# Attention and two expert layers on one core: value rows of two units summed on GpSimd, and eight group sums moved in VectorE's queue

## The chip, the cores and the metric

The program runs on one core of a Trainium2 chip. A time is the device time of one execution, in microseconds (us). The engines go by the profile's names: PE is TensorE's matmuls and PEld its weight loads, DVE is VectorE, ACT is ScalarE, POOL is GpSimd, and SP is SyncE, which here only issues transfers. Each engine works through its own queue of instructions in the order that was fixed when the program was built; an instruction that waits holds up all that stand behind it on its engine.

## The reference

Attention over 4 batches, 8 heads, 576 positions, 64 columns per head, is the sum of two parts. The first works on means over groups of four positions (144 groups) and is repeated four times along the sequence; the second sees only keys less than four positions away. The result goes through a dense layer (512 to 2048 to 512 with a squared ReLU) and through eight experts of which each token takes the best one.

```python
q_d = q.reshape(B, H, Sd, factor, D).mean(axis=3)   # k_d and v_d alike, factor 4
out_d = sm_attn(q_d, k_d, v_d)
out_up = np.repeat(out_d, factor, axis=2)
mask = np.abs(pos[:, None] - pos[None, :]) < factor
...
out_local = np.matmul(attn, v)
return (out_up + out_local).astype(np.float32)
```

## The kernel before, in words

**Units.** A unit is one batch and one pair of heads: `attention(b, hp, ap, psa)`, lines 195 to 342, a generator that is driven step by step. Its steps, as far as they matter here: load q and k (L198); the group sums of q and k, two `tensor_reduce` on VectorE (L205); load the value windows and the grouped value rows `vr` (L212, L214), local scores on TensorE (L226), mask (L233); scores of the groups (L242), maximum (L253), subtraction on GpSimd (L254), exponential on ScalarE (L255); maxima and sums (L262 to L270), the reciprocals of the sums (L271), the multiplication by them on GpSimd (L272); transposes `pt` on TensorE (L288) and their copy (L291); transposes `pdt` (L300) and their copy (L306); the product `pu` with the grouped values (L316) and its copy `up` (L321); the product `po` with the value windows (L329); and `xT`, the sum of both (L335 on VectorE).

**Grouped values.** The mean over four value rows is made in one of two ways. For batches 1 to 3 GpSimd adds the four rows in two instructions (L295, L296), and `pu` takes 8 matmuls. For batch 0 nothing is added; `pu` runs over all four rows, 32 matmuls, and PSUM's accumulation makes the sum.

**Order.** Four sets of buffers exist; set i does batch 0 and then batch 1 of head pair i (`serial`, L810). `rounds` (L830) drives the four sets in turn, set i starting i rounds late, and lets in the first pieces of the weight conversion (`f64_split`, L380: ScalarE L389, VectorE L390, L392, L394, ScalarE L396, GpSimd L397). Four such pieces are written ahead of the end of batch 0, later ones behind it, two for each chunk of the dense layer at first (`wanted`, L867). The order that each engine's queue gets is made from this written order by a planner that places an instruction when its inputs are there by its own reckoning; `tc.issue_after(x)` makes it keep an instruction behind x in the queue of x's engine, and adds no wait.

**Slots.** `pt`, `pdt`, `pu` and `po` of a unit take turns in two PSUM slots that units 0 and 1 share; units 2 and 3 have two others in batch 0. `po` of unit 1 takes the slot that `xT` of unit 0 empties.

**What follows.** The dense layer's first product (L461) takes `xT` of all four units of batch 0, split into two parts (L447, L448). From then on its matmuls (L461, L484), the rest of the conversion and the units of batch 1 run interleaved (L902 and on).

```python
parts = [(j, g) for j in range(2) for g in range(GR if b == 0 else 1)]
for j, g in parts:
    for a in range(2):
        nc.tensor.matmul(
            pu[64 * a:64 * a + 64, 0, 0:SD],
            lhsT=vr[:, a, j, g, :], rhs=PdT[:, j, :, a, :],
            start=((j, g) == parts[0]), stop=((j, g) == parts[-1]))
```

Of the kernel before, what the change touches and what calls it, by code (L numbers as in the profile page):

```python
# [16 lines left out]
ALU = mybir.AluOpType  # L17
AX = mybir.AxisListType
# [7 lines left out]
def attn_moe_kernel(  # L26
# [13 lines left out]
    nc = tc.nc  # L40
# [5 lines left out]
    P = 128  # L46
    GR = 4
    SD = S // GR
# [25 lines left out]
    class Parts:  # L74
# [32 lines left out]
        out=psum4, in_=ident.rearrange("p (k e) -> p e k", k=KC)[:, 0:2 * E, :], axis=AX.X, op=ALU.add)  # L107
# [80 lines left out]
    for o in orders:  # L188
        nc.gpsimd.dma_start(out=o.rearrange("(p c) o -> p (c o)", p=P), in_=none)
    nc.gpsimd.dma_start(out=ytab[0:1, :].rearrange("o (p c) -> (o p) c", p=8),  # L190
                        in_=none[0:8, 0:YW // 8])

    xT = {}

    def attention(b, hp, ap, psa):
        n = f"{b}_{hp}"
        qkt = ap.tile([P, 2, S], F32, tag="qk", name=f"qk{n}", bufs=2)
# [3 lines left out]
        qk_d = ap.tile([P, 2, SD + 16], F32, tag="qkd", name=f"qkd{n}")  # L201
        if b == 0:
            nc.gpsimd.memset(qk_d[:, 0, SD:], 0.0)
        for i in range(2):
            nc.vector.tensor_reduce(  # L205
                out=qk_d[:, i, 0:SD], in_=qkt[:, i, :].rearrange("p (s g) -> p s g", g=GR),
                axis=AX.X, op=ALU.add)
            yield

        def values():  # L210
# [10 lines left out]
        for ip in range(5):  # L221
            for x in range(2):
                for a in range(2):
                    hb = (x + a) % 2
                    i = 2 * ip + hb
# [6 lines left out]
        for a in range(2):  # L232
            nc.vector.scalar_tensor_tensor(  # L233
                out=sm[:, :, a, :], in0=ps[:, a, 0:320].rearrange("p (i c) -> p i c", i=5),
# [16 lines left out]
        smv = sm.rearrange("p i a c -> p (i a) c")  # L251
# [9 lines left out]
        sums, inv = st[:, 0:13], st[:, 13:26]  # L261
# [3 lines left out]
        for i in range(3):  # L265
# [2 lines left out]
                                 accum_out=sums[:, 10 + i:11 + i])  # L268
        nc.vector.tensor_reduce(out=sums[:, 0:10], in_=smv, axis=AX.X, op=ALU.add)
        nc.vector.tensor_scalar(out=sums, in0=sums, scalar1=1e-9, scalar2=None, op0=ALU.add)  # L270
        nc.vector.reciprocal(out=inv, in_=sums)  # L271
        nc.gpsimd.tensor_mul(out=smv, in0=smv,  # L272
                             in1=inv[:, 0:10].unsqueeze(2).to_broadcast([P, 10, 64]))
        yield
        if b == 0:
            for i in range(3):
# [2 lines left out]
        else:  # L279
            nc.gpsimd.tensor_mul(out=sd, in0=sd,  # L280
                                 in1=inv[:, 10:13].unsqueeze(2).to_broadcast([P, 3, SD]))
# [8 lines left out]
        PT = ap.tile([P, 5, P], F32, tag="PT", name=f"PT{n}")  # L290
        nc.scalar.activation(out=PT.rearrange("p i r -> p (i r)"), in_=ptv, func=AF.Copy)  # L291
        yield
        if b > 0:
            vq = vr.rearrange("p a j g d -> p (a j) g d")
            nc.gpsimd.tensor_add(out=vq[:, :, 0:2, :], in0=vq[:, :, 0:2, :], in1=vq[:, :, 2:4, :])  # L295
            nc.gpsimd.tensor_add(out=vq[:, :, 0, :], in0=vq[:, :, 0, :], in1=vq[:, :, 1, :])  # L296
        pt = psa.tile([P, 2, 512], F32, tag="at", name=f"pdt{n}")
        for j in range(2):
            for bi in range(3):
                nc.tensor.transpose(out=pt[:72, j, P * bi:P * bi + P],  # L300
                                    in_=sd[:, bi, 72 * j:72 * j + 72], identity=ident)
        if b < 2:
            PdT = ap.tile([72, 2, 3, 2, 48], F32, tag="sm", name=f"PdT{n}")
        else:
            PdT = ap.tile([72, 2, 3, 2, 48], F32, tag="PdT", name=f"PdT{n}")
        nc.scalar.activation(  # L306
            out=PdT.rearrange("p j b a c -> p j (b a) c"),
            in_=pt[:72, :, 0:3 * P].rearrange("p j (x c) -> p j x c", c=64)[:, :, :, 0:48],
# [1 line left out]
        yield  # L310

        pu = psa.tile([P, 2, 512], F32, tag="at", name=f"pu{n}")
        parts = [(j, g) for j in range(2) for g in range(GR if b == 0 else 1)]
        for j, g in parts:
            for a in range(2):
                nc.tensor.matmul(  # L316
# [8 lines left out]
        for i in range(NW):  # L325
            bk, o, ln = i // 5, Q0[i] - SH * (i // 5), Q0[i + 1] - Q0[i]
            r = (i % 2) * 64 + Q0[i] - QS[i]
            for a in range(2):
# [7 lines left out]
            out=xt.rearrange("p (h s g) -> p h s g", h=2, g=GR),  # L336
            in0=po[:, :, 0:SH].rearrange("p h (s g) -> p h s g", g=GR),
            in1=up.rearrange("p (h s) -> p h s", h=2).unsqueeze(3).to_broadcast(
                [P, 2, SD // 2, GR]),
            op=ALU.add)  # L340
# [3 lines left out]
    def chain(units):  # L344

        gens = [attention(*u) for u in units]

        def go(i, n):
            for _ in range(n if i < len(gens) else 0):
                next(gens[i], None)  # L350
                yield

        yield from go(0, 4)
        for i in range(len(gens)):
            yield from go(i, 3)
            yield from go(i + 1, 3)
            yield from go(i, 2)
            yield from go(i + 1, 1)
            yield from go(i, 1)
            if len(gens) == 1:  # L360
                yield from gens[i]
            else:
                go_on = gens[i]
                next(go_on, None)
                yield
# [444 lines left out]
    def serial(units):  # L810
        gens = [attention(*u) for u in units]
        next(gens[0])
        yield
        for i, g in enumerate(gens):
            for n, _ in enumerate(g):
                if n == 2 and i + 1 < len(gens):
                    next(gens[i + 1])
                yield
# [83 lines left out]
    for s in range(len(seq) + LAG):  # L902
        if s < len(seq):
            sg, c, f = seq[s]
            j, n = f - SEGS[sg][1], SEGS[sg][2] - SEGS[sg][1]
# [52 lines left out]
    with tc.high_priority():  # L958
# [11 lines left out]
        for i in range(2):  # L970
            nc.gpsimd.indirect_dma_start(
                out=xg01[i][:], out_offset=None, in_=ytab[:],
# [6 lines left out]
    for o in orders:  # L979
        og = cv.tile([P, DM], I32, tag="tmp", name="og", bufs=TMPB).bitcast(F32)[:E * NTL // 2, 0:2 * P]  # L980
        nc.gpsimd.dma_start(out=og.rearrange("t (h p) -> t h p", h=2),
                            in_=o.rearrange("(t h p) o -> t h (p o)", h=2, p=P))
# [31 lines left out]
    for h in range(2):  # L1014
        nc.vector.tensor_sub(out=sh[:, h], in0=pov[:, h, :, 1:HT], in1=gih[:, h, :, 0:HT - 1])
        nc.vector.tensor_tensor(out=sh[:, h], in0=sh[:, h],
                                in1=star.unsqueeze(2).to_broadcast([P, E, HT - 1]),
                                op=ALU.mult)
        nc.vector.tensor_tensor(out=gih[:, h, :, 0:HT - 1], in0=pov[:, h, :, 0:HT - 1], in1=sh[:, h],
                                op=ALU.add)  # L1020
# [203 lines left out]
```

## Time and profile before

| | |
|---|---|
| median of 3 runs | 903.58 us (902.75 to 905.36) |
| the profiled execution | 903.22 us |
| its span, first to last instruction | 901.4 us |
| PE busy | 821.4 us, 91% of the span |
| DVE, ACT, POOL busy | 450.6, 395.3, 341.6 us |
| mean granted TensorE clock | 0.973 of full speed |

The profiled execution lies 0.36 us under the median; 1.8 us of it lie outside the span. The shares are means over stages that differ: batch 0's attention takes the first 67 us, after which the dense layer's matmuls run.

### The profile page before, as it was taken

The page shows a single profiled execution, that of the slowest core. Times are in us where ns is not written, and L with a number is a line of the kernel's source. Part 1 is how long each engine was busy: PE and PEld are TensorE (multiplying, and loading weights), DVE is VectorE, ACT ScalarE, POOL GpSimd, SP SyncE. Part 2 cuts the span into 40 slices and gives each one's busy share as a digit, 9 for nine tenths or more (in the row PEclk, how much of TensorE's full clock was granted, in tenths as well). Part 3 has the DMA queues.
Part 4 walks back from the last instruction along what each step waited for, and adds up shares of the span by engine and source line. Part 5 has one row for each costly group of instructions (what it writes and reads, how often), then busy time and mean ns, then how long its engine had stood idle before and what let it go on. Part 6 is the DMA issues. An engine that isn't in the chain of part 4 may idle for free. (4 is left out here: it accounts for less than half of the span.)

```text
span 901.4 us, 15844 instructions
## 1 busy us (share of the span) xinstructions
PE 821.4 (91%) x5983; PEld 695.4 (77%) x5983; DVE 450.6 (50%) x961; ACT 395.3 (44%) x899; POOL 341.6 (38%) x411
## 2 busy tenths in 40 slices
PE   4598979997899989999999999997799989999996
PEld 3386869886788878888988888775587767878785
DVE  8987585777354654353222224652743656434121
ACT  3644555554434443344333324552643656444221
POOL 4556454454344445453323232413422332221111
PEclk9989989999899999999999999998899999999999
DMA  9750321454034332010000031635945594431111
GB/s 335 254 179 31 117 80 71 164 187 163 24 102 79 79 101 65 30 38 30 1 25 1 1 95 55 207 110 152 355 148 191 172 347 137 177 132 37 49 35 35
DMA packets 35519, 103.45 MB, mean 115 GB/s; under 512 B 6836, under 2 KB 6864, under 8 KB 35408
## 3 DMA queue, kind: packets, MB, share of 16 engines
q1 hardware_dynamic: 30000, 87.16, 28.9%
q0 software_dynamic: 5408, 14.88, 5.4%
q8 instruction: 61, 1.00, 0.5%
q14 instruction: 50, 0.41, 0.2%
HBM read 88.16 MB, written 14.65 MB: 114 GB/s over the span
## 5 line engine op out<-in xcount | busy, mean ns | idle before, releaser
L461 PE MATMUL ph<-xc,win 128*128 128x256 f32 x1728 | 244.6, 288 | 14.1 <-DVE g L466 11.9
L461 PEld LDWEIGHTS ph<-xc,win 128*128 128x128 f32 x1728 | 230.0, 193 | 33.4 <-DVE g L466 14.8
L484 PE MATMUL y<-wout,gs 128*128 128x512 f32 x864 | 233.0, 401 | 5.0 <-ACT gs L469 4.1
L470 POOL TENSOR_TENSOR gs<-g,gs 128x256 fp32r<-128x256 f32 x144 | 111.8, 780 | 201.1 <-ACT gs L469 123.7
L484 PEld LDWEIGHTS y<-wout,gs 128*128 128x128 f32 x864 | 152.7, 190 | 34.8 <-ACT gs L469 5.1
L466 DVE SCALAR_TENSOR_TENSOR g<-ph,g 128x256 f32<-128x256 f32 x144 | 60.2, 420 | 173.0 <-ACT g L465 172.8
L465 ACT ACTIVATE g<-ph 128x256 f32<-128x256 f32 x144 | 54.7, 382 | 121.7 <-PE ph L461 101.2
L469 ACT ACTIVATE gs<-g 128x256 fp32r<-128x256 f32 x144 | 59.5, 415 | 60.5 <-DVE g L466 55.1
L794 PE MATMUL ph<-we_wa,xs 128*128 128x512 f32 x228 | 64.3, 417 | 16.2 <-PEq L1155 10.7
L1041 POOL DMA_INDIRECT xg<-ytab,apt x23 | 33.2, 1442 | 88.2 <-ACT apt L799 44.4
L794 PEld LDWEIGHTS ph<-we_wa,xs 128*128 128x128 f32 x228 | 42.4, 195 | 28.4 <-ACT we_wd L657 11.1
L794 PE MATMUL ph<-we_wb,xs 128*128 128x512 f32 x228 | 60.3, 399 | 0.6 <-issue 0.6
L1082 DVE COPY g<-g 128x2 f32<-128x2 f32 x19 | 3.2, 168 | 104.0 <-ACT ob L1073 104.0
L1069 PE MATMUL py<-we_wc,hs 128*128 128x512 f32 x216 | 54.2, 399 | 0.0
L1069 PE MATMUL py<-we_wd,hs 128*128 128x512 f32 x216 | 53.4, 396 | 0.0
L794 PEld LDWEIGHTS ph<-we_wb,xs 128*128 128x128 f32 x228 | 43.6, 191 | 11.7 <-issue 1.1
L1073 ACT ACTIVATE ob<-py,g 128x512 f32<-128x512 f32 x18 | 12.4, 687 | 88.4 <-PE py L1069 78.5
L1076 POOL DMA_INDIRECT out_dram<-ob,oi x18 | 18.6, 1034 | 82.6 <-issue 36.2
L1069 PEld LDWEIGHTS py<-we_wd,hs 128*128 128x128 f32 x216 | 40.6, 188 | 9.8
L1069 PEld LDWEIGHTS py<-we_wc,hs 128*128 128x128 f32 x216 | 39.8, 188 | 8.7
L799 ACT ACTIVATE apt<-ph 128x512 f32<-128x512 f32 x38 | 22.9, 601 | 45.2 <-PE ph L794 45.2
L448 DVE TENSOR_TENSOR xc<-xT,xc 128x256 fp32r<-128x256 f32 (+3 forms) x76 | 37.0, 537 | 2.8 <-ACT xc L447 2.8
(258 smaller groups left out, 1217.4 us busy)
## 6 DMA issues: line engine op xcount, KB each, us to landing
apt<-in_w_dram SPq DMA_DIRECT2D x37, 512.0 KB, 3.1
stg<-in_w_dram SPq DMA_DIRECT2D x35, 512.0 KB, 7.6
apt<-in_qk_dram SPq DMA_DIRECT2D x10, 576.0 KB, 4.3
raw<-in_w_out_dram SPq DMA_DIRECT2D x11, 512.0 KB
raw<-in_w_in_dram SPq DMA_DIRECT2D x11, 512.0 KB, 3.3
ytab<-yr SPq DMA_DIRECT2D x18, 260.0 KB, 2.3
yr<-ypart SPq DMA_DIRECT2D x8, 512.0 KB, 4.2
sparewb<-in_qk_dram SPq DMA_DIRECT2D x6, 576.0 KB, 13.1
```

The costliest lines, as they stand in the source:

```text
L448: nc.vector.tensor_sub(out=t[:, 1, hp, done:done + ln], in0=src, in1=hi.bitcast(F32))
L461: nc.tensor.matmul(ph, lhsT=wv[:, wh, kk, :], rhs=x[:, xh, kk, :], start=(n == 0), stop=(n == 3 * KC - 1))
L465: nc.scalar.activation(out=g, in_=ph, func=AF.Relu)
L466: nc.vector.scalar_tensor_tensor(out=g, in0=ph, scalar=0.0, in1=g, op0=ALU.max, op1=ALU.mult)
L469: nc.scalar.activation(out=gs[:, 0, :], in_=g, func=AF.Copy)
L470: nc.gpsimd.tensor_sub(out=gs[:, 1, :], in0=g, in1=gs[:, 0, :].bitcast(F32))
L484: nc.tensor.matmul(yps[c][i], lhsT=gs[:, gh, P * i:P * i + P], rhs=woutv[f // FQ][:, f % FQ, wh, :], start=(first and n == 0), stop=(last ...
L794: mm = nc.tensor.matmul(ph, lhsT=xs[:, a, P * kk:P * kk + P], rhs=w1v(b, kk)[:, 512 * h:512 * h + 512], start=(n == 0), stop=(n == 3 * KC ...
L799: nc.scalar.activation(out=hr[:, 512 * h:512 * h + 512], in_=ph, func=AF.Relu)
L1041: nc.gpsimd.indirect_dma_start(out=xg[:], out_offset=None, in_=ytab[:], in_offset=bass.IndirectOffsetOnAxis(ap=idx, axis=0))
L1069: nc.tensor.matmul(py, lhsT=hs[:, a, P * kf:P * kf + P], rhs=w2v(b, kf), start=(kf == 0 and n == 0), stop=(kf == KF - 1 and n == 2))
L1076: nc.gpsimd.indirect_dma_start(out=out, out_offset=bass.IndirectOffsetOnAxis(ap=oi[:, 0:1], axis=0), in_=ob[:], in_offset=None, bounds_che ...
```

## The change

Three things are edited. The two sums of q and of k of each batch-1 unit are kept behind a reciprocal of batch 0 in VectorE's queue: the last one that was written by then, which is that of unit 3. Units 0 and 1 of batch 0 get GpSimd's two additions of value rows, kept behind the first multiplication by reciprocals (unit 0's) in GpSimd's queue. Their `pu` then takes 8 matmuls in place of 32; units 2 and 3 of batch 0 keep 32.

```diff
         for i in range(2):
-            nc.vector.tensor_reduce(
-                out=qk_d[:, i, 0:SD], in_=qkt[:, i, :].rearrange("p (s g) -> p s g", g=GR),
-                axis=AX.X, op=ALU.add)
+            with ExitStack() as behind:
+                if b == 1:
+                    behind.enter_context(tc.issue_after(marks["inv"]))
+                nc.vector.tensor_reduce(
+                    out=qk_d[:, i, 0:SD], in_=qkt[:, i, :].rearrange("p (s g) -> p s g", g=GR),
+                    axis=AX.X, op=ALU.add)
             yield
...
-        nc.vector.reciprocal(out=inv, in_=sums)
-        nc.gpsimd.tensor_mul(out=smv, in0=smv,
-                             in1=inv[:, 0:10].unsqueeze(2).to_broadcast([P, 10, 64]))
+        rc = nc.vector.reciprocal(out=inv, in_=sums)
+        ml = nc.gpsimd.tensor_mul(out=smv, in0=smv,
+                                  in1=inv[:, 0:10].unsqueeze(2).to_broadcast([P, 10, 64]))
+        if b == 0:
+            marks["inv"] = rc.ins
+            marks.setdefault("mul", ml.ins)
...
-        if b > 0:
+        pooled = b > 0 or hp < 2
+        if pooled:
             vq = vr.rearrange("p a j g d -> p (a j) g d")
-            nc.gpsimd.tensor_add(out=vq[:, :, 0:2, :], in0=vq[:, :, 0:2, :], in1=vq[:, :, 2:4, :])
-            nc.gpsimd.tensor_add(out=vq[:, :, 0, :], in0=vq[:, :, 0, :], in1=vq[:, :, 1, :])
+            with ExitStack() as behind:
+                if b == 0:
+                    behind.enter_context(tc.issue_after(marks["mul"]))
+                nc.gpsimd.tensor_add(out=vq[:, :, 0:2, :], in0=vq[:, :, 0:2, :],
+                                     in1=vq[:, :, 2:4, :])
+                nc.gpsimd.tensor_add(out=vq[:, :, 0, :], in0=vq[:, :, 0, :], in1=vq[:, :, 1, :])
...
-        parts = [(j, g) for j in range(2) for g in range(GR if b == 0 else 1)]
+        parts = [(j, g) for j in range(2) for g in range(1 if pooled else GR)]
```

## Rows read from the trace of the kernel before

**Rows 1.** Stages: window, length, busy us PE, PEld, DVE, ACT, POOL, then PEclk, DMA share, GB/s
```profile
23.60:41.80 18.20, 7.11 (x37) 5.22 (x37) 18.16 (x33) 11.95 (x32) 10.64 (x8) 1.00 0.80 262
41.80:54.10 12.30, 10.52 (x125) 9.30 (x121) 9.01 (x12) 7.46 (x15) 7.72 (x6) 1.00 0.55 181
54.10:67.12 13.02, 12.98 (x252) 11.62 (x252) 11.47 (x18) 4.14 (x11) 7.14 (x8) 0.74 0.57 168
67.12:128.00 60.88, 49.80 (x595) 41.87 (x589) 44.92 (x82) 31.20 (x87) 32.77 (x32) 0.96 0.23 78
```
**Rows 2.** Timeline of PE: start us, length us, line and tiles, [idle before <-releaser]
```profile
37.36 1.33 PE L288 MATMUL pt<-ident,sparewc 128*128 128x128 f32 x5 [7.11 <-POOL sparewc L272]
...
40.29 4.11 PE L316 MATMUL pu<-apt 72*64 72x144 f32 x32
...
47.86 1.38 PE L329 MATMUL po<-apt 64*64 64x60 f32 x40
49.17 2.18 PE L316 MATMUL pu<-sparewc 72*64 72x144 f32 x32
...
54.14 2.23 PE L329 MATMUL po<-sparewd,sparewb 64*64 64x60 f32 x40 [1.82 <-DVE xT L335]
...
65.94 0.79 PE L242 MATMUL ds<-apt 64*64 64x144 f32 x10
...
127.91 2.50 PE L461 MATMUL ph<-xc,win 128*128 128x256 f32 x10 [4.88 <-DVE g L466]
```
**Rows 3.** Timeline of DVE from the first reciprocal to the last of batch 0
```profile
23.60 0.22 DVE L271 RECIPROCAL apt<-apt 128x13 f32<-128x13 f32 x1
23.74 1.34 DVE L205 TENSOR_REDUCE apt<-apt 128x144 f32<-128x576 f32 x2
...
28.86 1.40 DVE L205 TENSOR_REDUCE sparewb<-sparewb 128x144 f32<-128x576 f32 x2
...
31.63 1.26 DVE L270 TENSOR_SCALAR sparewc<-sparewc 128x13 f32<-128x13 f32 x1
...
33.53 0.16 DVE L270 TENSOR_SCALAR sparewc<-sparewc 128x13 f32<-128x13 f32 x1
33.61 1.40 DVE L205 TENSOR_REDUCE sparewb<-sparewb 128x144 f32<-128x576 f32 x2
...
35.60 0.32 DVE L271 RECIPROCAL sparewc<-sparewc 128x13 f32<-128x13 f32 x2
...
41.56 0.24 DVE L271 RECIPROCAL sparewc<-sparewc 128x13 f32<-128x13 f32 x1
```
**Rows 4.** Timeline of DVE from there to xT of unit 0
```profile
43.62 1.09 DVE L390 TENSOR_SCALAR cvt<-cvt 128x512 int32<-128x512 int32 x1 [1.81 <-ACT cvt L389]
...
46.08 0.42 DVE L390 TENSOR_SCALAR cvt<-cvt 128x512 int32<-128x512 int32 x1
46.53 0.69 DVE L392 SCALAR_TENSOR_TENSOR cvt<-sparewd,cvt 128x512 int32<-128x512 int32 x1
...
50.18 1.38 DVE L390 TENSOR_SCALAR cvt<-cvt 128x512 int32<-128x512 int32 x1 [1.27 <-ACT cvt L389]
...
52.73 0.69 DVE L394 SCALAR_TENSOR_TENSOR cvt<-sparewd,cvt 128x512 int32<-128x512 int32 x1
53.34 0.75 DVE L335 TENSOR_TENSOR xT<-po,apt 128x576 f32<-128x576 f32 x1
```
**Rows 5.** Timeline of POOL
```profile
25.68 1.71 POOL L272 TENSOR_TENSOR apt<-apt 128x640 f32<-128x640 f32 x1
31.60 1.26 POOL L397 TENSOR_TENSOR win<-cvt,win 128x512 fp32r<-128x512 f32 x1 [4.20 <-ACT win L396]
33.69 1.26 POOL L254 TENSOR_TENSOR sparewc<-sparewc 128x640 f32<-128x640 f32 x1 [0.83 <-DVE sparewc L270]
...
62.17 1.27 POOL L295 TENSOR_TENSOR sparewc<-sparewc 72x512 f32<-72x512 f32 x1 [0.97 <-DMA sparewc<-in_vgrp_dram]
63.52 0.73 POOL L296 TENSOR_TENSOR sparewc<-sparewc 72x256 f32<-72x256 f32 x1
```

More of the change, by code (lines that the diff above doesn't have):

```diff
@@ L193, in attn_moe_kernel @@
     xT = {}
+    marks = {}
     def attention(b, hp, ap, psa):
```

## The prediction, made before the changed kernel ran

> **What bounds the kernel now.** I read three views in this order: the table of stages, to see which engine is full where; the timelines of TensorE (PE) and VectorE (DVE) over the first 70 us; and the bracket at the end of each row, which says who ended an engine's idle time.
>
> The stages first [rows 1]. Between 23.60 and 41.80 us VectorE is busy for 18.16 of 18.20 us, TensorE for 7.11: this stage belongs to VectorE's queue. From 41.80 to 54.10 TensorE is busy for 10.52 of 12.30 and VectorE for 9.01, so here they wait for each other. [...]
>
> The link between the first two stages is the row at 37.36: TensorE stood idle for 7.11 us until GpSimd's multiplication (L272) was done for the transposes of unit 1 [rows 2]. That multiplication needs the reciprocal of unit 1, which VectorE runs at 35.60 together with unit 2's; unit 3's follows at 41.56 [rows 3]. Ahead of the 35.60 row stand three pairs of batch 1's group sums, at 23.74, 28.86 and 33.61; a fourth pair stands between 35.60 and 41.56 [rows 3]. TensorE first asks for these sums with batch 1's group scores at 65.94 [rows 2]; they merely stand early in the queue.
>
> The second link is `xT` of unit 0. Its matmuls `po` end at 47.86 + 1.38 = 49.24 us [rows 2], but VectorE reaches L335 only at 53.34, after two pauses of 1.81 and 1.27 us for ScalarE's part of the weight conversion [rows 4]. TensorE then waits 1.82 us with `po` of unit 1 for that `xT` (its slot) and starts it at 54.14 [rows 2].
>
> **The change part by part.**
>
> *Group sums behind the reciprocal.* All four pairs leave the stretch before unit 3's reciprocal. For units 1 and 2 three of them count: 1.34 + 1.40 + 1.40 = 4.1 us less in the queue ahead of 35.60 [rows 3]. The work is not saved; it comes back behind unit 3's reciprocal, still ahead of `xT` of unit 0. No transfer is issued by a moved sum; their cover is the time from 41.56 to the scores at 65.94, some 24 us [rows 2, 3], and if it failed each late pair would cost its 1.4 us.
>
> *Additions on GpSimd.* Two units at 1.27 + 0.73 = 2.0 us [rows 5] are 4.0 us. Behind unit 0's multiplication at 25.68 GpSimd is idle for 4.20 us until 31.60 [rows 5], so they nearly fill one hole. What is late next is what stands behind them: the subtraction L397 at 31.60 and unit 3's L254. They also put a new wait before `pu` of units 0 and 1: in the hole they end at 27.4 + 4.0 = 31.4, well before the 40.29 of unit 0's `pu` [rows 2], so I count it at nothing; placed late, they would hold that `pu` and, behind it on TensorE, the transposes `pdt` and all of units 1 to 3. What they can cost is VectorE's time. The trace has the case: L270 took 1.26 us at 31.63, beside GpSimd's L397 of 1.26 us, and 0.16 us at 33.53 with GpSimd idle [rows 3, 5]. The group sums at 33.61 took 1.40 us beside GpSimd's L254, as the pair at 28.86 did alone [rows 3, 5], so reductions are not held. The cost therefore lies between 0 (reductions stand beside the additions) and 4.0 (each addition holds VectorE for its whole length). I take the middle, 2.0, since reductions and instructions like L270 alternate in this stretch [rows 3]; both ends stay for the range.
>
> [...]
>
> So the reciprocals of units 1 and 2, and with them the transposes at 37.36, come 4.1 - 2.0 = 2.1 us earlier.
>
> *Shorter `pu`.* Unit 0's takes 4.11 us for 32 matmuls [rows 2]; 8 at that pace take 1.03, so 3.1 us go. TensorE runs without a pause from 40.29 to past 49.24, so `po` of unit 0 ends 2.1 + 3.1 = 5.2 us earlier, at 44.0. Unit 1's `pu` shrinks from 2.18 [rows 2] to a quarter, 0.55, but what follows it on TensorE is the wait for `xT`; I count this 1.6 us at nothing, hidden by that wait, and if the wait vanishes it is a gain more.
>
> *`xT` of unit 0.* For TensorE's 5.2 us to arrive, VectorE has to reach L335 5.2 us earlier although the additions hold it for 2.0 us more: 7.2 us to find. Its queue holds 1.81 + 1.27 = 3.1 us of pauses, and conversions of 0.42 + 0.69 + 0.69 = 1.8 us each on VectorE [rows 4]. Eight of them have ended by 53.34 (counted by their L394, the last at 52.73 [rows 4]), of which only four are written ahead of `xT`; the planner put the other four in while `xT` was not ready. With `po` done 5 us earlier I estimate that two of them fall behind: 3.1 + 3.6 = 6.7, and `xT` comes 6.7 - 2.0 = 4.7 us earlier.
>
> *From there on.* TensorE is full from 54.10 to 67.12 [rows 1], so the 4.7 us pass to the dense layer's start. The two conversions put behind cost VectorE 3.6 us between 67 and 128 us, where it is idle for 60.88 - 44.92 = 16 us [rows 1]. Transfers of batch 1's `vr` wait on SP for the `pu` of batch 0 and come earlier with it; the conversion's loads wait for L394 and shift with the conversions. I count both at zero; the later idle time, such as the 4.88 us at 123 to 127.9 us [rows 2], moves along with its causes.
>
> **The sum.** 903.22 - 4.7 = 898.5 us for the profiled execution. The median stands 0.36 us above that execution, so I forecast 898.9 us. A measurement of this kernel tells about 0.3% (2.7 us) from no change.
>
> **The rivals.**
>
> *A, paid back later (no change).* The conversions that fall behind are missed at 123 us: the wait of 4.88 us there ends with VectorE's L466 [rows 2], so VectorE's queue is the late one. If the 3.6 us come back there, 4.7 - 3.6 = 1.1 us remain: 902.5. For it: this wait. Against it: VectorE's 16 us of idle time before. That the change does not do what it says belongs here too: `issue_after` only keeps an order, and a planner that had the sums behind the reciprocal but a conversion in their place would win nothing.
>
> *B, VectorE held by the additions (slower).* The place is `xT` of unit 0, and the point is whether it ends later than now, 54.09 us. If every addition holds VectorE (4.0 us), no conversion falls behind, and the pauses stay because ScalarE's L389 waits for GpSimd's L397, which the additions push back, `xT` comes 2.0 to 4.0 us later and TensorE's 3.1 + 1.6 us only lengthen the wait before 54.14. Over the median that is 905.6 to 907.6, 906.6 in the middle. For it: the 1.26 against 0.16 us, and a stage in which VectorE has no idle time. Against it: the hole of 4.20 us on GpSimd and the four pairs of sums, some 5.5 us, that no longer stand in that stage.
>
> [...]
>
> *C, more than that.* Nothing is held (2.0 more), unit 1's `pu` counts (1.6 more), and the stage from 54.10 to 67.12 no longer runs at 0.74 of the clock, because the pause of 1.82 us ahead of it is gone: up to 0.26 x 13.0 = 3.4 us more [rows 1, 2]. That makes 8.3 to 11.7 in place of 4.7: 891.9 to 895.3.
>
> **How the numbers follow.** Forecast 0.47, A 0.22, B 0.15, C 0.16. The forecast's own range is 896.9 to 900.9: the unknown 2.0 us of being held, either way. The range that should hold 8 in 10 reaches from 892.5 (most of C) to 906.0 (A and the nearer part of B). Faster by over 0.3% means below 900.9: the forecast and C, 0.63. Within 0.3%: A, 0.22. Slower: B, 0.15.
>
> **What would show it.** In the profile after: the pairs of L205 of batch 1 behind the third row of L271; L295 and L296 of units 0 and 1 in GpSimd's hole after 27 us; the first `pt` of unit 1 at about 35.3 (a row still at 37 breaks the first step); `pu` of unit 0 with 8 matmuls in about 1.0 us; `xT` of unit 0 at about 48.6; L461 first at about 62.4 in place of 67.12. If L394 or L390 take 1.3 us and more beside L295, the price of 2.0 was too low. If L461 starts 4.7 us earlier but the wait at 123 us grows by as much, A is right. If the stage before L461 still shows 0.74, C is out.

## The result, and the profile after

The changed kernel is slower. Its median is 912.71 us over 9 runs (909.28 to 915.68), against 904.05 us over 9 runs of before on the same chip: a ratio of 1.0095, 95% interval 1.0072 to 1.0117. Measured a second time, the same kernel gave 1.0066 (1.0044 to 1.0088). The forecast was 898.9 us, its range ended at 906.0. The profiled execution took 910.97 us, 7.75 us more than that of before.

**Stages.** The table of stages over the same four windows as [rows 1]:

```profile
23.60:41.80 18.20, 7.78 (x37) 5.55 (x35) 16.69 (x26) 11.31 (x32) 15.53 (x13) 0.50 0.84 263
41.80:54.10 12.30, 11.25 (x109) 9.18 (x110) 10.34 (x16) 6.18 (x16) 5.81 (x6) 0.59 0.33 101
54.10:67.12 13.02, 7.00 (x200) 6.47 (x196) 12.33 (x14) 5.03 (x12) 9.12 (x10) 0.94 0.92 298
67.12:128.00 60.88, 52.76 (x612) 44.28 (x612) 44.28 (x82) 30.19 (x85) 32.21 (x31) 0.87 0.19 66
```

In the third window TensorE, full before, is busy for 7.00 of 13.02 us, while VectorE has hardly any room left (12.33). GpSimd went from 10.64 to 15.53 us in the first window.

**TensorE.** Its timeline, for [rows 2]:

```profile
34.86 1.33 PE L296 MATMUL pt<-ident,sparewc 128*128 128x128 f32 x5 [4.37 <-POOL sparewc L277]
...
39.21 1.23 PE L329 MATMUL pu<-apt 72*64 72x144 f32 x8
42.85 1.33 PE L296 MATMUL pt<-ident,sparewc 128*128 128x128 f32 x5 [2.41 <-POOL sparewc L277]
44.10 3.62 PE L329 MATMUL pu<-sparewc,sparewc 72*64 72x144 f32 x26
47.66 1.50 PE L313 MATMUL pdt<-ident,sparewc 128*72 128x128 f32 x6
49.09 2.39 PE L342 MATMUL po<-apt 64*64 64x60 f32 x40
...
59.03 1.33 PE L342 MATMUL po<-sparewd,sparewc 64*64 64x60 f32 x40
...
71.35 0.87 PE L231 MATMUL ls<-sparewb 64*64 64x64 f32 x18 [10.25 <-issue]
72.15 3.00 PE L474 MATMUL ph<-xc,win 128*128 128x256 f32 x10
```

The early rows came as forecast: the transposes at 34.86 in place of 37.36, `pu` of unit 0 in 1.23 us in place of 4.11. The last `po` of batch 0 ends at 60.36 us. Then TensorE stands still for 10.25 us, and the dense layer (now L474) starts at 72.15 in place of 67.12.

**VectorE.** Its timeline, for [rows 3, 4] and beyond:

```profile
23.53 0.22 DVE L276 RECIPROCAL apt<-apt 128x13 f32<-128x13 f32 x1
...
29.75 0.22 DVE L276 RECIPROCAL sparewc<-sparewc 128x13 f32<-128x13 f32 x1
29.89 3.80 DVE L403 TENSOR_SCALAR cvt<-cvt 128x512 int32<-128x512 int32 x1
...
35.97 0.22 DVE L276 RECIPROCAL sparewc<-sparewc 128x13 f32<-128x13 f32 x1
...
51.52 0.76 DVE L348 TENSOR_TENSOR xT<-po,apt 128x576 f32<-128x576 f32 x1 [1.01 <-PE po L342]
...
62.09 3.75 DVE L461 TENSOR_TENSOR xc<-xT,xc 128x256 fp32r<-128x256 f32 x2
65.77 0.68 DVE L405 SCALAR_TENSOR_TENSOR cvt<-raw,cvt 128x512 int32<-128x512 int32 x1
66.48 1.64 DVE L407 SCALAR_TENSOR_TENSOR cvt<-raw,cvt 128x512 int32<-128x512 int32 x1
...
69.76 0.69 DVE L407 SCALAR_TENSOR_TENSOR cvt<-raw,cvt 128x512 int32<-128x512 int32 x1
70.37 0.88 DVE L238 SCALAR_TENSOR_TENSOR apt<-ls,mask 128x320 f32<-128x320 f32 x2
...
72.02 0.75 DVE L348 TENSOR_TENSOR xT<-po,sparewc 128x576 f32<-128x576 f32 x1
```

Two things are new. At 29.89 one conversion (L403, the old L390, 0.42 us in [rows 4]) takes 3.80 us. And between 65.77 and 70.45 the ninth and tenth weight conversions stand in front of the mask of batch 1's unit 0 (L238) and of `xT` of unit 3 (L348), whose `po` had been done since 60.36. That mask empties the PSUM slot that TensorE's scores at 71.35 write, so TensorE's 10.25 us are a wait for VectorE's queue. The view names no releaser ("issue"), but the mask ends at 71.25, 0.10 us before the scores start, and in the second profile of the change and in the three repaired kernels further down the same two times lie 0.09 or 0.10 us apart. In before all ten conversions were done by 60.2 us.

**GpSimd.** Its timeline beside the 3.80 us, for [rows 5]:

```profile
27.80 1.27 POOL L307 TENSOR_TENSOR apt<-apt 72x512 f32<-72x512 f32 x1
29.02 1.27 POOL L307 TENSOR_TENSOR sparewc<-sparewc 72x512 f32<-72x512 f32 x1
30.25 1.26 POOL L410 TENSOR_TENSOR win<-cvt,win 128x512 fp32r<-128x512 f32 x1
31.47 0.73 POOL L309 TENSOR_TENSOR apt<-apt 72x256 f32<-72x256 f32 x1
32.15 1.26 POOL L259 TENSOR_TENSOR sparewc<-sparewc 128x640 f32<-128x640 f32 x1
33.36 1.45 POOL L277 TENSOR_TENSOR sparewc<-sparewc 128x640 f32<-128x640 f32 x1
34.77 0.72 POOL L309 TENSOR_TENSOR sparewc<-sparewc 72x256 f32<-72x256 f32 x1
```

The additions (L307, L309) are there, but there is no hole any more: with the group sums gone, the subtraction (L259) and the multiplication (L277) are ready earlier too, and GpSimd works back to back from 27.80 to 35.49. The second unit's reciprocal was done at 29.97, but its multiplication stands behind the additions in GpSimd's queue and starts only at 33.36. The transposes at 34.86 are thus held by GpSimd's queue and not by VectorE's.

**Further down.** I follow the lead by marks that every kernel has (us):

| profiled execution | first dense matmul | first store of the dense result | last store | first expert copy | last expert copy |
|---|---|---|---|---|---|
| before | 67.12 | 99.25 | 606.52 | 657.78 | 894.87 |
| the change | 72.15 | 103.59 | 611.32 | 662.28 | 902.61 |

The 4.3 us lost by the first store are still 4.8 at the last one and 4.5 at the first expert. The experts add 3.2 more, in one place: the eighth interval between their copies takes 17.0 us in place of 13.3; all others agree within 0.8 us, in both directions. So two losses are to be explained: some 4.5 us in the front, 3.7 us at 763 us.

### The profile page after: what moved, and what is told of

The parts are those of the page before. It is cut to its first block, busy times and chain, and to the rows that moved or that the text cites. A ratio compares the mean times of both kernels' runs of the same rounds, so it can differ in the third digit from the quotient of the medians.

```text
span 909.2 us, 15745 instructions
## 1 busy us (share of the span) xinstructions
PE 822.4 (90%) x5935; PEld 695.6 (77%) x5935; DVE 452.3 (50%) x961; ACT 393.9 (43%) x899; POOL 346.2 (38%) x415
## 3 DMA queue, kind: packets, MB, share of 16 engines
q8 instruction: 62, 1.02, 0.5%
## 5 line engine op out<-in xcount | busy, mean ns | idle before, releaser
L474 PE MATMUL ph<-xc,win 128*128 128x256 f32 x1728 | 247.9, 291 | 12.4 <-DVE g L479 9.3
L474 PEld LDWEIGHTS ph<-xc,win 128*128 128x128 f32 x1728 | 233.1, 195 | 31.6 <-DVE g L479 10.6
L483 POOL TENSOR_TENSOR gs<-g,gs 128x256 fp32r<-128x256 f32 x144 | 113.7, 792 | 201.3 <-ACT gs L482 132.5
L1054 POOL DMA_INDIRECT xg<-ytab,apt x23 | 28.4, 1236 | 92.7 <-ACT apt L812 44.4
L461 DVE TENSOR_TENSOR xc<-xT,xc 128x256 fp32r<-128x256 f32 (+3 forms) x76 | 39.1, 563 | 2.8 <-ACT xc L460 2.8
```

The costliest lines, as they stand in the source:

```text
L461: nc.vector.tensor_sub(out=t[:, 1, hp, done:done + ln], in0=src, in1=hi.bitcast(F32))
L474: nc.tensor.matmul(ph, lhsT=wv[:, wh, kk, :], rhs=x[:, xh, kk, :], start=(n == 0), stop=(n == 3 * KC - 1))
L483: nc.gpsimd.tensor_sub(out=gs[:, 1, :], in0=g, in1=gs[:, 0, :].bitcast(F32))
L1054: nc.gpsimd.indirect_dma_start(out=xg[:], out_offset=None, in_=ytab[:], in_offset=bass.IndirectOffsetOnAxis(ap=idx, axis=0))
```

## The experiments

In what follows "first store" and so on are the columns above; ratios are against before on the same chip.

**One half at a time.** The first kernel moves the sums and adds nothing on GpSimd for batch 0:

```diff
-        pooled = b > 0 or hp < 2
+        pooled = b > 0
```

> Only the group sums are moved; units 0 and 1 keep 32 matmuls and nothing is added on GpSimd. Queue theory (TensorE gains about 6 us by 60 us, and loses them because the ninth and tenth weight conversions now stand in VectorE's queue ahead of unit 3's xT and of the mask of batch 1's unit 0): here xT of unit 3 has one conversion fewer ahead of it, so first dense matmul at 66 to 69 us, total within 3 us of before. Rival, moved sums are the loss (5.5 us of sums behind 41 us push everything on VectorE): as slow as the change, first dense matmul at 71 to 73 us, total 909 or more.

Measured: 901.8 us, ratio 0.9978 (0.9954 to 1.0002); marks 64.50, 97.10, 603.11, 653.86, 891.07; eighth interval 13.3. The second kernel keeps the additions and leaves the sums where they were:

```diff
-                if b == 1:
-                    behind.enter_context(tc.issue_after(marks["inv"]))
+                pass
```

> Only the additions on GpSimd with 8 matmuls for units 0 and 1; the group sums stay where they were. Queue theory: in this order ten conversions stand ahead of xT of unit 2, a little worse than before and better than the change: first dense matmul at 65 to 70 us, total 901 to 908. Rival, GpSimd's additions hold VectorE and that is the loss: first dense matmul at 71 us or later, total 909 or more.

Measured: 904.5 us, ratio 0.9988 (0.9966 to 1.0011); marks 67.74, 96.73, 603.94, 656.69, 896.85; eighth interval 17.2. Neither half is slower than before; at the last store they are 3.4 and 2.6 us ahead. The loss in the front belongs to the two together. (The sums alone did better than expected, in the start and in the total; the additions alone fell inside what was expected.)

**The order in front of the dense layer.** The ninth and tenth conversions are kept behind `xT` of unit 3:

```diff
-            f64_split(raw, dst[:, 0], dst[:, 1])
+            with ExitStack() as behind:
+                if i >= 8:
+                    behind.enter_context(tc.issue_after(marks["xt"]))
+                f64_split(raw, dst[:, 0], dst[:, 1])
```

> The change, with VectorE's part of the ninth and later conversions kept behind unit 3's xT. Queue theory: mask of batch 1's unit 0 at about 62 us and xT of unit 3 at about 63 in place of 70.4 and 72.0, TensorE's idle stretch of 10.25 us shrinks to under 4, first dense matmul at 63 to 66 us, total 6 to 9 us below the change, so about 903 to 906. Rival, the clock or code loading on TensorE is the loss: idle stretch stays 8 us or more, total within 2 us of the change.

Measured: 910.39 us, 1.005 (1.0029 to 1.007); marks 65.56, 101.66, 610.61, 662.1, 902.52; eighth interval 17.2. The start came as expected, the total did not: of the 6.6 us gained at the start 1.9 are left at the first store. Another kernel keeps batch 1's additions behind the copies into `carry` on GpSimd instead:

```diff
+                if b == 1:
+                    behind.enter_context(tc.issue_after(marks["carry"]))
...
-        nc.gpsimd.tensor_copy(carry[:, hp, :], xT[0, hp][:, 2 * CH:S])
+        marks["carry"] = nc.gpsimd.tensor_copy(carry[:, hp, :], xT[0, hp][:, 2 * CH:S]).ins
```

> The change, with GpSimd's additions of batch 1 kept behind the copies that follow batch 0's xT. Queue theory, VectorE's side: the two conversions still stand ahead of xT of unit 3, but the splits of xT are no longer held by those additions (3.75 us for two splits in the change), so first dense matmul at 67 to 70 us, total 2 to 5 us below the change. Rival, the conversions alone matter: first dense matmul at 71 us or later, total within 2 us of the change.

Measured: 909.3 us, 1.0057 (1.0027 to 1.0087); marks 65.73, 100.25, 607.35, 660.02, 899.62; eighth interval 17.0. Here both conversions still stand in front of the mask, and yet the dense layer starts as early as with them moved: the two splits of `xT` that take 3.75 us at 62.09 in the change, beside batch 1's additions on GpSimd, take 1.81. The conversions are only a part of what held the mask. And a kernel with both edits:

> The change, with the conversions from the ninth on behind unit 3's xT and GpSimd's additions of batch 1 behind the copies that follow batch 0's xT. Queue theory: TensorE's 5.9 us of gain reach the dense layer, first dense matmul at 60 to 64 us and no pause of more than 2 us behind it before 72 us; with the stall in the expert stage still there, total 898 to 903. Rival, clock or code loading in the front: dense layer still starts at 67 us or later, total 907 or more.

Measured: 908.62 us, 1.0034 (1.0014 to 1.0053); marks 62.78, 98.71, 608.39, 660.74, 901.01; eighth interval 17.0. TensorE's timeline, the first row that of the conversions' kernel, the others those of the kernel with both edits:

```profile
65.10 0.53 PE L231 MATMUL ls<-sparewb 64*64 64x64 f32 x18 [3.31 <-issue]
```

```profile
62.32 0.53 PE L231 MATMUL ls<-sparewb 64*64 64x64 f32 x18 [1.56 <-issue]
62.78 1.32 PE L481 MATMUL ph<-xc,win 128*128 128x256 f32 x9
65.61 0.58 PE L481 MATMUL ph<-xc,win 128*128 128x256 f32 x1 [1.50 <-ACT xc L467]
...
68.27 0.80 PE L481 MATMUL ph<-xc,win 128*128 128x256 f32 x2 [1.46 <-DVE xc L468]
...
75.44 2.29 PE L481 MATMUL ph<-xc,win 128*128 128x256 f32 x9 [2.90 <-DVE g L486]
```

The wait of 10.25 us was VectorE's queue: it falls to 3.31 and 1.56 us as the work ahead of the mask goes (4.89 with the additions alone moved). The dense layer then starts at 62.78, where the prediction had it (62.4), but the lead isn't kept. What was put behind is late next: 1.50, 1.46 and 2.90 us of new waits, the last two for VectorE's `xc` and `g`. Of 4.3 us ahead at the start 0.5 are left at the first store, and at the last store the kernel is 1.9 behind. The total of 898 to 903 us that was expected did not come.

**TensorE's instruction count.** The pause at 763 us has no releaser; "issue" is time for which the profile shows none. The change has 48 matmuls fewer (5935 in place of 5983) and 48 weight loads fewer ahead of that place: 96 instructions. The theory is that TensorE waits there for code (the page of the change lists 62 and 50 packets, 1.02 and 0.41 MB, in two queues of the kind "instruction"), because its instructions now fall elsewhere in it. No row shows that; the runs below test it. The rival is that the pause comes with the later or other schedule. The first trial put 48 tiny fp32 matmuls ahead of the first local scores:

```diff
+        if b == 0 and hp == 0:
+            for _ in range(48):
+                nc.tensor.matmul(ps[0:64, 0, 0:4], lhsT=ident[0:64, 0:64], rhs=ident[0:64, 0:4],
+                                 start=True, stop=True)
```

> The change, with 48 tiny matmuls put ahead of the first local scores on TensorE, where it is idle anyway, so that TensorE's instruction count is that of before. Queue theory for the first 360 us: dense layer starts 4 to 5 us late as in the change. For the rest of the loss (about 3.5 us that the change loses in the expert stage, at a pause of TensorE for nothing that the profile shows while expert weights stream in): if it hangs on where TensorE's instructions fall in its code, the expert stage takes as long as before and the total is 3 to 5 us below the change; if not, total within 1.5 us of the change.

Measured: 905.41 us, 0.9999 (0.9978 to 1.002); marks 69.33, 103.23, 611.78, 663.95, 900.63; eighth interval 13.3. The pause is gone, but each fp32 matmul came out as two loads and two matmuls (6031 in all, 48 above before), and the planner put the front in another order, so this run alone decides little. The same matmuls were then put into the first transposes of the experts, where the front stays as it is; 48 into the change, and 80 into before, to see whether the pause comes with another count there:

```diff
+        if name == "0_0":
+            for _ in range(48):
+                nc.tensor.matmul(px[0:64, 0:4], lhsT=ident[0:64, 0:64], rhs=ident[0:64, 0:4],
+                                 start=True, stop=True)
```

> The change, with 48 tiny matmuls put into the first transposes of the expert stage, behind the dense layer, so that the order of everything before it is unchanged and TensorE's instruction count is that of before from there on. Code-position theory (the expert stage of the change loses 3.5 us in one interval, 17.0 in place of 13.3 us, because TensorE reaches a new stretch of code just as expert weights stream in): that interval is 13.3 us again, the total is 3 to 4 us below the change. Rival, the stall follows the late start of the dense layer: interval 17 us, total within 1 us of the change or up to 2 us slower for the added matmuls.

Measured: 916.37 us, 1.0131 (1.011 to 1.0152); eighth interval 13.3.

> The kernel before, with 80 tiny matmuls put into the first transposes of the expert stage; nothing else changed, order up to there as before. [...] Rival: all intervals as before, total 0 to 3 us above before for the added matmuls.

Measured: 921.28 us, 1.0184 (1.0163 to 1.0205); eighth interval 13.2. Again twice the instructions meant: +96 and +320 against before. Both totals lie above what was expected, because the added matmuls alone took 7.74 and 14.28 us. In bf16 each came out as one load and one matmul (5983 matmuls in all with 48 in the change), and the counts are the intended ones (`lhsT=ones[0:32, 0:32], rhs=ones[0:32, 0:4]` in the same place): 48 in the change, which restores before's count, and 80 in before, which lies 256 instructions above the change.

> The change with 48 tiny bf16 matmuls (each one weight load and one matmul, so exactly the 96 instructions that the change takes away) in the first transposes of the expert stage; order up to there as in the change. Code-position theory: no interval of 17 us in the expert stage, 13.3 in its place, and, the tiny matmuls costing 1.5 to 4 us, total 0 to 3 us below the change. Rival, the stall belongs to the change's late start: interval 17 us and total 1.5 to 4 us above the change.

Measured: 911.56 us, 1.0072 (1.0052 to 1.0092); marks 72.69, 104.10, 612.84, 665.65, 901.78; eighth interval 13.3.

> [...] Front: the program is that of before up to 600 us, so the first dense matmul here (67.1 in the first profile, 70.8 in the second) shows how far it moves from execution to execution.

Measured: 912.7 us, 1.0082 (1.0055 to 1.0109); marks 68.06, 100.15, 608.54, 665.72, 903.75; eighth interval 14.8. The change once more, beside them:

> The change itself once more, for a second profile on the same chip as its variants. Queue theory: first dense matmul at 70 to 73 us, behind an idle stretch of TensorE of 9 us or more that ends with the mask of batch 1's unit 0 on VectorE; interval of 17 us in the expert stage again. If the first dense matmul is at 67 to 69, the late start of the first profile was an accident of that execution. Total 909 to 914.

Measured: 911.69 us, 1.0066 (1.0044 to 1.0088); marks 72.78, 104.41, 614.02, 666.22, 906.16; eighth interval 17.1. The late start is there again. The idle stretch before it is 7.23 us, less than expected, because the last `po` of batch 0 ended only at 64.00; VectorE was busy for 8.83 of the 13.02 us of the third window here, where the first profile has 12.33. TensorE's timelines at that place, of the change, of the change with the count restored, and of before with 80 more:

```profile
762.53 0.97 PE L807 MATMUL ph<-we_wa,xs 128*128 128x512 f32 x3 [0.93 <-ACTq L1169]
765.59 1.65 PE L807 MATMUL ph<-we_wa,xs 128*128 128x512 f32 x3 [2.10 <-issue]
```

```profile
765.45 1.66 PE L807 MATMUL ph<-we_wa,xs 128*128 128x512 f32 x6 [0.92 <-ACTq L1173]
```

```profile
765.86 0.96 PE L794 MATMUL ph<-we_wa,xs 128*128 128x512 f32 x3 [0.92 <-ACTq L1160]
768.11 0.97 PE L794 MATMUL ph<-we_wa,xs 128*128 128x512 f32 x3 [1.29 <-issue]
```

The same group of six is cut after the third matmul in the two programs that lie 256 instructions apart, and it runs whole with before's count. Over all kernels, with TensorE's instructions against before: at -96 six programs of six have 17.0 to 17.2 us, with a pause of 1.91 to 2.12 us (the change, both of its repairs and their union, the additions alone, the change again); at +160 14.8; at 0, +96 and +320 nine of nine, with before and the kernels told of further down, have 13.2 to 13.3. So the pause goes with TensorE's instruction count, and neither with the late start (the additions alone have it at a start of 67.74, the change with the count restored lacks it at 72.69) nor with the change's order (before with 160 instructions more has one). At +160 the pause is shorter, and the granted clock behind it stays at 1.00; in the change it is 0.58 from 765.59 to 769.15 us, which by estimate (0.42 x 3.56 = 1.5 us) makes most of the rest of the 3.7 us.

That loading of code makes the pause is not shown. The DMA view of the change, 761.5 to 764.5 us, has the two queues of the kind "instruction":

```profile
q14 instruction: 3, 0.02, 2.7%
q8 instruction: 1, 0.02, 2.5%
```

The one packet of q8 (0.02 MB) falls between 762.5 and 763.0 us, just before the pause (763.50 to 765.59), and the loads of the next expert's weights begin at 763.41. But the view of before, 757.5 to 760.5 us, around the same group of six (758.50 to 760.16), has the same packets, that of q8 between 759.0 and 759.5 us, and no pause:

```profile
q14 instruction: 3, 0.02, 2.2%
q8 instruction: 1, 0.02, 2.1%
```

Which engine the packets are for the views don't say. The two counts that have the pause, -96 and +160, lie 256 instructions apart. If it comes back at a fixed distance, these runs can't tell 256 from 128, of which 256 is a multiple too (64 is out: -96 and +96 are 192 apart, and only one has the pause). What lies at such a distance is not shown either.

The missing pause is no gain in the total, though: the kernel with the count restored lies level with the change (911.56 and 911.69 us). The tiny matmuls took 1.35 us themselves and its first expert copy came at 665.65. The pause is shown by the interval, not by the medians.

**Everything put right.** Both order edits and the 48 bf16 matmuls:

> The change with conversions from the ninth on behind unit 3's xT, batch 1's additions behind the copies after batch 0's xT, and the 48 tiny bf16 matmuls in the expert stage. Queue and code-position theories together: first dense matmul at 61 to 65 us, no interval of 17 us, total 902 to 907 (the tiny matmuls cost 1.5 to 4 us of it). Rival: total 909 or more.

Measured: 908.5 us, 1.0028 (1.0011 to 1.0046); marks 62.52, 98.45, 608.24, 661.42, 898.38; eighth interval 13.2. It is still above before, and above the 902 to 907 us that were expected.

**The half that pays.** The sums alone were measured again, and once more with batch 1's additions behind `carry`:

> Only the group sums are moved, no additions for batch 0, a second measurement. If moving the sums alone is worth something, the dense layer starts at 64 to 65.5 us in place of 67.1 and the milestones up to the last store of the dense layer's result stay 2 to 3.5 us ahead, ratio 0.996 to 0.998 with the upper end under 1.000. If the first measurement was only a lucky stretch of the clock, the ratio lies within 0.001 of 1. TensorE's instructions are as many as before, so the interval in the expert stage is 13.2 to 13.4 us.

Measured: 900.6 us over 9 runs (898.26 to 903.63) against 905.84: 0.9948 (0.993 to 0.9965); marks 65.73, 97.27, 602.99, 655.5, 891.96; eighth interval 13.3.

> The sums moved, no additions for batch 0, and batch 1's additions kept behind the copies into carry on GpSimd. If the early additions of batch 1 hold VectorE's subtractions and masks in front of the dense layer, the first dense matmul comes another 1 to 2 us earlier than with the sums alone (62.5 to 63.5 us). If what is won there is paid back by batch 1's later units, the first store of the dense layer's result still comes no earlier than with the sums alone (97 us) and the ratio is that of the sums alone, 0.998. Interval in the expert stage 13.2 to 13.4 us, as TensorE's count is that of before.

Measured: 900.52 us, 0.9949 (0.9925 to 0.9973); marks 66.65, 101.44, 605.58, 658.23, 895.31 (the profiled execution took 903.73 us, more than that median); eighth interval 13.3. The sums alone are faster than before in the second measurement; the first one leans the same way, but its interval reaches 1.0002. They stand at 0.9948 where the change stands at 1.0066 and 1.0095. Moving batch 1's additions away changes nothing in the total, and the earlier start that was expected of it (62.5 to 63.5 us) did not come.

**What the halves do to each other.** VectorE in the repeated sums-only kernel, the reciprocals of the first three units in its order, with `xT` of unit 0, and GpSimd's row at the place of the hole:

```profile
24.06 0.22 DVE L276 RECIPROCAL apt<-apt 128x13 f32<-128x13 f32 x1
...
30.28 0.22 DVE L276 RECIPROCAL sparewc<-sparewc 128x13 f32<-128x13 f32 x1
...
33.58 0.23 DVE L276 RECIPROCAL sparewc<-sparewc 128x13 f32<-128x13 f32 x1
...
47.50 0.76 DVE L348 TENSOR_TENSOR xT<-po,apt 128x576 f32<-128x576 f32 x1
```

```profile
29.10 1.27 POOL L410 TENSOR_TENSOR win<-cvt,win 128x512 fp32r<-128x512 f32 x1 [0.73 <-ACT win L409]
```

Between the second and the third lie 3.30 us; in the change it is 35.97 - 29.75 = 6.22, with the same instructions between them. That is the additions' price on VectorE here: 2.9 us. In the kernel with the additions alone they meet something else, shown by GpSimd's and then VectorE's timeline:

```profile
29.32 1.27 POOL L306 TENSOR_TENSOR sparewc<-sparewc 72x512 f32<-72x512 f32 x1
30.55 0.72 POOL L308 TENSOR_TENSOR apt<-apt 72x256 f32<-72x256 f32 x1
```

```profile
24.34 0.22 DVE L275 RECIPROCAL apt<-apt 128x13 f32<-128x13 f32 x1
...
29.59 1.40 DVE L209 TENSOR_REDUCE sparewb<-sparewb 128x144 f32<-128x576 f32 x2
30.91 0.92 DVE L406 SCALAR_TENSOR_TENSOR cvt<-sparewd,cvt 128x512 int32<-128x512 int32 x1
...
36.56 0.32 DVE L275 RECIPROCAL sparewc<-sparewc 128x13 f32<-128x13 f32 x2
...
48.11 0.75 DVE L347 TENSOR_TENSOR xT<-po,apt 128x576 f32<-128x576 f32 x1
```

The pair of group sums takes its 1.40 us beside an addition, unheld, and the conversion behind it 0.92 in place of 0.69. Counted from the start of the first reciprocal to the end of the third, the four kernels compare as follows (us):

| | sums in their old place | sums moved |
|---|---|---|
| no additions | 12.32 (before) | 9.75 |
| additions | 12.54 | 12.66 (the change) |

Beside the sums the additions cost 0.2 us; without them 2.9, and all that the moved sums had gained is gone. The sums were the cover of the additions, and the other half of the change moves them away.

## Why the prediction was wrong

**The sums' move: right.** Alone, it brings the transposes of the second unit to 33.17 us in the repeated sums-only kernel, 4.2 us earlier than in [rows 2]; the prediction had 4.1 for it. The two measurements put its worth at 0.2 and 0.5% of the run.

**The price of the additions: sized from rows that the change itself removes.** The bounds were 0 and 4.0 us, and the middle was taken "since reductions and instructions like L270 alternate in this stretch". That was true of before. The same diff takes all eight batch-1 reductions out of the stretch, so the additions meet instructions that are held (L403 at 29.89, 3.80 us in place of 0.42); 2.9 us was measured where 2.0 was taken. The size alone would have changed the sum by 0.9. The cover "hole of 4.20 us" failed as well: the hole was there because GpSimd's next work waited, by way of ScalarE, for VectorE, and the moved sums made that work ready. In the sums-only kernel the hole is 0.73 us. That the transposes came at 34.86, close to the 35.3 forecast, is luck: the step had them follow the reciprocal, which was 5.9 us earlier than in [rows 3], and what they waited for was the multiplication behind the additions in GpSimd's queue.

**`po` and `xT` of unit 0: failed.** Forecast 44.0 for the end of `po`, measured 51.48; 48.6 for `xT`, measured 51.52 [rows 2, 4]. The step read "TensorE runs without a pause from 40.29 to past 49.24" as a fixed order. In the change the planner put a `pt` that waited 2.41 us for GpSimd, 26 matmuls of another unit's `pu` and a `pdt` between the short `pu` and `po`, and `po` itself took 2.39 us in place of 1.38 (granted clock 0.50 and 0.59 in the first two windows). Of the 4.7 us counted for `xT`, 1.8 came; either half alone brings more, 5.8 and 5.2.

**"The 4.7 us pass to the dense layer's start": the step that decided.** TensorE did finish batch 0 earlier, 60.36 in place of 66.10 us. But the prediction counted how many conversions fall behind `xT` of unit 0 and not where they land. They landed in front of batch 1's first mask and of `xT` of unit 3, behind splits that took 3.75 us beside batch 1's additions, in a stage where VectorE, at 11.47 of 13.02 us [rows 1], had 1.6 us to spare; the idle 16 us that were to take them come only after 67 us. Put behind that point too, the conversions cost new waits on VectorE, as rival A had it, at 65 to 75 us rather than at 123. The halves show that the step fails by itself: `xT` of unit 0 comes 5.8 us earlier with the sums alone and 5.2 with the additions alone, and the dense layer starts 1.4 us earlier and 0.6 us later.

**The experts' 3.7 us: in no step and no rival.** The prediction put taking instructions away at nothing for all that stands behind them; the pause goes with their number, and how it comes about is open.

**The rivals.** B named VectorE held by GpSimd and a slower kernel, and both came, but not at its place: `xT` of unit 0 was earlier than before, not later than 54.09. A's mechanism, VectorE's work missed later, shows in the new waits of the repaired kernels; that it is all that kept them from winning is not shown. C is out: the third window ran at 0.94 of the clock (0.78 in the second profile), as C had hoped, with TensorE idle for 6 of its 13 us.

**What stays open.** Where the repaired kernel with the count restored loses the rest (1.7 us behind before at the last store, 3.5 at the last expert copy) is not settled. Nor is how much of the front's 4 to 5 us is order and how much is clock. The granted clock of a window can't tell: in the change with the count restored it reads 1.00 in the first two windows, and `po` of unit 0 takes 2.39 us there too. One front, with the same instructions in the same order, doesn't always take the same time: before and the two kernels that only add matmuls to it in the experts started the dense layer at 67.12, 68.06 and 70.76 us, the change and its likes at 70.82, 72.15, 72.69 and 72.78. The means lie 3.5 us apart, where the two first profiles show 5.0, and the latest of the one kind (70.76) all but meets the earliest of the other (70.82).

## What to carry to other kernels

When a diff has two parts, price each in the schedule that the other leaves, and measure them apart: here the work that one part moved was the cover on which the other's price rested, and one part alone was the better kernel. For each piece of work that "falls behind", name the instruction in front of which it lands and what waits for that one; idle time later in the queue is no cover for a place that has none. And after a change in the number of an engine's instructions, look for new pauses without a releaser far behind the change.

## What was not expected of the hardware

- One VectorE instruction of 0.4 us took 3.80 us, from 29.89 to 33.69: past the ends of three GpSimd instructions (30.29, 31.51 and 32.20), to about that of a fourth (33.41). They came without a gap. That they held it is a reading of these times; no row says how. In [rows 3, 5] an instruction beside one of GpSimd's took 1.1 us more (1.26 in place of 0.16).
- A `tensor_reduce` beside an addition was not held: a pair took 1.40 us in the kernel with the additions alone, as it did in before.
- 96 instructions fewer on TensorE made a pause of 2.1 us and an interval 3.7 us longer, 700 us later; before with 160 more, 256 above the change, has a pause (1.29 us) at the same matmul.
